# GpSimd's two additions of x's halves in eight pieces, and the last output tile's second product in two pieces of columns

## The chip, the cores and the metric

The kernel runs on one core of a Trainium2 chip. The metric is the device time of one execution in microseconds (us). Engine names are those of the profile: PE is TensorE, PEld its weight loads, DVE is VectorE, ACT is ScalarE, POOL is GpSimd, and SP is the engine that issues most of the DMAs.

## What is computed

An attention layer with a learned position bias (2 batches, 8 heads, 576 positions, head size 64) is followed by a mixture of 4 experts over the 1152 tokens. Cut to what matters:

```python
def _moe_ref(x, domain_probs, w1, w2):      # x: (1152, 512), the attention's output
    p = domain_probs / (domain_probs.sum(-1, keepdims=True) + 1e-09)
    out = np.zeros((N, D), dtype=np.float32)
    for e in range(E):                       # w1[e]: (512, 1024), w2[e]: (1024, 512)
        h = np.maximum(x @ w1[e], 0.0)
        out += p[:, e:e + 1] * (h @ w2[e])
    return out
```

## The kernel before, in words

The program has two parts, each planned by the class `Plan`: a list of operations with engine, cost, due time and dependences, from which a simulated run writes one fixed order per engine. Every engine then works through its own list in that order; it does not skip an instruction that has to wait.

The first part (to about 218 us) is attention. For each of nine tiles of 128 tokens it makes x, and keeps it as two f16 halves, `xx[:, 0]` (the rounded value) and `xx[:, 1]` (what the rounding lost). The part ends with the first product of the first half-expert ("unit" u = 0): `mm1` (L475 to L477) on two groups of 384 tokens, c = 0 and 1, with four blocks of 128 hidden columns ("ft") each. A block of the result goes through one of three rotating buffers `hf`: ScalarE's `ev_a` (L480, L481) writes relu(h) to `hf` and its f16 value to `hh`, and VectorE's `ev_v` (L484) subtracts the two for the low half. A block's `ev_a` thus needs the `ev_v` of the block three before it. On VectorE these eight subtractions stand in one queue with the preparation of the next unit's weights: scales (L268 to L272), gate (L452), `whi` (L459) and two `wlo` (L463).

The second part (`plan_experts`) makes the second product of unit 0 (`mm2`, L497 to L499), the rest of its first product, and units 1 to 7, whose first product is taken in seven block products from sums of x and of w (`prod`, L594). For the sums of x, GpSimd first adds the two halves of x to one f32 array `xf` (in the trace `xsf`): `x_whole` (L547), one instruction for 640 tokens by 4 blocks of 128 features (128x2560 elements) and one for 512 tokens (128x2048). VectorE's `x_sums` (L544) read all of it. Behind `x_whole` GpSimd makes the sums of w for unit 1 (`w_sums`, L574, four instructions of 512 columns).

`mm2(u, tau)` makes one output tile: 4 blocks ft, 3 matmuls each (high by high, high by low, low by high), into one PSUM bank of 512 columns. `sum_up` (L504 for u = 0, else L506) multiplies by the gate and adds on VectorE; after unit 7 `store` (L512) writes the tile's 128 rows of 512 f32 to HBM. The last tile is unit 7, tau = 8.

Of the kernel before, what the change touches and what calls it, by code (L numbers as in the profile page):

```python
# [12 lines left out]
ALU = mybir.AluOpType  # L13
# [3 lines left out]
B, H, S, D = 2, 8, 576, 64  # L17
NF = 32
E, DM, FF = 4, 512, 1024
P = 128  # L20
NTAU = 9
# [4 lines left out]
NU = 8  # L26
# [129 lines left out]
def tile_attention_moe(ctx: ExitStack, tc: tile.TileContext, qd, kd, vd, cst, ltab, dp, mw1, mw2, out):  # L156
    nc = tc.nc
    V, A, G, T, SP = nc.vector, nc.scalar, nc.gpsimd, nc.tensor, nc.sync
# [11 lines left out]
    gate = keep.tile([P, NTAU, E], F32, name="gate")  # L170
    gs = keep.tile([P, NTAU, 1], F32, name="gs")
    gu = keep.tile([P, 2, NTAU], F32, name="gu")
# [8 lines left out]
    xx = keep.tile([P, 2, 4, NT], F16, name="xx")  # L181
# [12 lines left out]
    xf = pa.tile([P, 512], F32, name="xf")  # L194
# [17 lines left out]
    buf = {}  # L212
# [181 lines left out]
    moe = {"raw": [raw[:, 0], raw[:, 1]], "w": [wa]}  # L394
# [70 lines left out]
    def wpart(u, m, l):  # L465
        return moe["w"][u % 2][:, m].rearrange("p (l k f) -> p l k f", l=2, k=4)[:, l]

    def hpart(u, c, l):
        return hh_[:, (3 * u + c) % 2].rearrange("p (l k t) -> p l k t", l=2, k=4)[:, l]
# [13 lines left out]
    def ev_v(u, c, ft, ps, f):  # L483
        V.tensor_tensor(out=hpart(u, c, 1)[:, ft], in0=f, in1=hpart(u, c, 0)[:, ft], op=ALU.subtract)  # L484

    def mm2(u, tau, ps):
        if u:
            i = tau // 5
            hh, hl = hpair(i, 0), hpair(i, 1)
            ts = slice(P * (tau - 5 * i), P * (tau - 5 * i) + P)  # L490
        else:
            c, tt = divmod(tau, 3)
            hh, hl = hpart(u, c, 0), hpart(u, c, 1)
            ts = slice(P * tt, P * tt + P)
        wh, wl = wpart(u, 1, 0), wpart(u, 1, 1)
        for ft in range(4):
            T.matmul(ps, hh[:, ft, ts], wh[:, ft], start=(ft == 0), stop=False)  # L497
            T.matmul(ps, hh[:, ft, ts], wl[:, ft], start=False, stop=False)  # L498
            T.matmul(ps, hl[:, ft, ts], wh[:, ft], start=False, stop=(ft == 3))  # L499

    def sum_up(u, tau, ps):
        g, acc = gu[:, u % 2, tau:tau + 1], moe["acc"][:, tau]
        if u == 0:
            V.tensor_scalar(out=acc, in0=ps, scalar1=g, scalar2=None, op0=ALU.mult)  # L504
        else:
            V.scalar_tensor_tensor(out=acc, in0=ps, scalar=g, in1=acc, op0=ALU.mult, op1=ALU.add)  # L506

    def store(tau):
        acc = moe["acc"][:, tau]
        if tau:  # L510
            r = (tau - 1) % 2 * S + (tau - 1) // 2 * P
            SP.dma_start(out=out[r:r + P], in_=acc)  # L512
        else:
            for b in range(B):
                SP.dma_start(out=out[b * S + 512:b * S + S], in_=acc[64 * b:64 * b + 64])
# [14 lines left out]
    def hpair(i, l):  # L530
        return moe["hp"][i][:, l]

    def tokens(i, t=None):
        o, n = PAIRS[i]
        return slice(o, o + 2 * n) if t is None else slice(o + n * t, o + n * t + n)

    def x_sums(i):

        f = moe["xf"]

        def q(t, a):
            return f[:, 2 * a:2 * a + 2, tokens(i, t)]

        return [lambda x=x: V.tensor_tensor(out=x[0], in0=x[1], in1=x[2], op=x[3]) for x in ((q(1, 1), q(1, 0), q(1, 1), ALU.add), (q(1, 0), q(0, 0), q(1, 0), ALU.subtract), (q(0, 0), q(1, 1), q(0, 0), ALU.subtract), (q(0, 1), q(0, 1), q(0, 0), ALU.subtract))]  # L544

    def x_whole(i):
        G.tensor_tensor(out=moe["xf"][:, :, tokens(i)], in0=xx[:, 0, :, tokens(i)], in1=xx[:, 1, :, tokens(i)], op=ALU.add)  # L547

    def x_halves(i, a, l):
        s = slice(2 * a, 2 * a + 2)  # L550
        f, xs = moe["xf"][:, s, tokens(i)], moe["xs"][:, :, s, tokens(i)]
        if l:
            V.tensor_tensor(out=xs[:, 1], in0=f, in1=xs[:, 0], op=ALU.subtract)
        else:
            A.activation(out=xs[:, 0], in_=f, func=AF.Copy)
# [40 lines left out]
    def plan_experts():  # L596
# [4 lines left out]
        buf = {}  # L601
        EV = -6.0

        def op(name, eng, at, cost, fn, choice=False, **kw):
            plan.add(name, name[0], at, (lambda e: fn(e)) if choice else (lambda e: fn()), cost=cost if choice else {eng: cost}, **kw)
# [33 lines left out]

        def second(u, tau, at):  # L640
            i = tau // 5
            if u:
                deps = [("lo", u, i, k) for k in range(8)] + ([("wlo", u, j) for j in range(2)] if u > 1 else [])
            else:
                deps = [("ev_v", ft) for ft in range(4)] if tau > 5 else []
            op(("mm2", u, tau), "T", at, 2.6, lambda: mm2(u, tau, buf["o", u, tau]), deps=deps, new=[("o", ("o", u, tau))])
            op(("sum", u, tau), "V", at + 2.6 + EV, 0.75, lambda: sum_up(u, tau, buf["o", u, tau]), deps=[("mm2", u, tau)] + ([("gate", u)] if u > 1 else []), use=[("o", u, tau)], after=[("sum", u - 1, tau)] if u else [])
            if u == NU - 1:
                op(("store", tau), "S", at, 1.0, lambda: store(tau), deps=[("sum", u, tau)])
# [47 lines left out]


        for i in range(2):
            op(("xw", i), "G", 6.0 * i, 6.0 - i, lambda i=i: x_whole(i))  # L700
            for k, fn in enumerate(x_sums(i)):
                op(("xs", i, k), "V", 1 + 12.0 * i + k, 0.85, fn, deps=[("xs", i, k - 1)] if k else [("xw", i)])
            for a in range(2):
                op(("xhh", i, a), "A", 4 + 12.0 * i, 1.2, lambda i=i, a=a: x_halves(i, a, 0), deps=[("xs", i, 3)])
                op(("xh", i, a), "V", 5 + 12.0 * i, 1.45, lambda i=i, a=a: x_halves(i, a, 1), deps=[("xhh", i, a)])
        for tau in range(6):
            second(0, tau, 2.6 * tau + (8 if tau > 2 else 0))
        for ft in range(4):
            at = 7.8 + 2 * ft
# [3 lines left out]
        for u in range(1, NU):  # L713
            weights(u)
            a0 = 42.0 * u - 18
            for q in range(2):
                quad(u, 0, q, a0 + 11 * q, 11 / 7.0)
                quad(u, 1, q, a0 + 22 + 10 * q, 10 / 7.0)
            last = range(6, NTAU) if u == 1 else range(5, NTAU)
            for k, tau in enumerate(last):  # L720
                second(u - 1, tau, a0 + 22.0 * (k + 1) / (len(last) + 0.5))
            for k in range(5):
                second(u, k, a0 + 22 + 20.0 * (k + 1) / 5.5 if u < NU - 1 else a0 + 42 + k)
# [44 lines left out]
    for tau in range(NTAU):  # L768
# [4 lines left out]
        for hp in range(HP):  # L773
            p = HP * tau + hp
            op("scores", (p,), 2 * p + PR["scores"], scores, p, deps=[("load_q", tau)] + [("load_k", b, hp) for b in batches], after=chain("scores", p) + [("bias_mm", 8 * block + 3)], new=[("b2", ("s", 2 * p)), ("b2", ("s", 2 * p + 1))], use=[("q", tau)], mode="row2" if tau else "quad")
            for h in range(2):
                u = 2 * p + h
# [4 lines left out]
        for g in range(9):  # L782
            ps = sorted({HP * tau + (4 * g + i) // 9 for i in range(4)})
            at = 2 * ps[-1] + (4 * g + 3) % 9 * 0.1
# [46 lines left out]
    for c in range(2):  # L831
        for ft in range(4):
            for kt in range(4):
                key = ("h", c, ft)
                prev = ("mm1", c, ft, kt - 1) if kt else ("mm1", c, ft - 1, 3) if ft else ("mm1", c - 1, 3, 3) if c else None
                op("mm1", (c, ft, kt), PR["mm1"] + 4 * c + ft, lambda c=c, ft=ft, kt=kt, key=key: mm1(0, c, ft, buf[key][:, 0:384], [kt]),
                   new=[] if kt else [("b1", key)], use=[key] if kt else [], after=[prev] if prev else [],
                   deps=[("xlo", 3 * c + i) for i in range(3)] + [("wlo", 0, j) for j in range(2)])
# [3 lines left out]
    with tc.manual_schedule():  # L842
        load_consts()
        warm()
        prep_consts()
        plan.run()
        plan.emit(buf)
        open_a()
        plan_experts()
# [68 lines left out]
```

## Time and profile before

| | |
|---|---|
| median of three runs (lowest to highest) | 566.19 us (565.79 to 566.46) |
| the profiled execution's own time | 566.17 us |
| its span in the trace | 564.4 us |
| busy share of PE, DVE, ACT, POOL | 96%, 72%, 52%, 26% |
| PE's share of the chain that ended last | 87% |

The span runs from the first to the last instruction of the trace, and 1.77 us of the execution's time lie around it. A row of the timeline gives start, duration, engine, line, operation, and in brackets how long the engine stood idle before it and what ended that. The duration of an instruction runs from its start on the engine to its end, and takes in what it waited for after it started.

### The profile page before, as it was taken

How to read it: one execution, taken by the hardware profiler on the slowest of the kernel's cores; microseconds unless marked ns; L12 is line 12 of the kernel's file. 1: busy time of each engine (PE TensorE's matmuls, PEld its weight loads, DVE VectorE, ACT ScalarE, POOL GpSimd, SP SyncE). 2: the span in 40 equal slices, each digit the busy share in tenths (PEclk: the TensorE clock that was granted, in tenths of full speed). 3: DMA queues.
4: the chain of work that ended last, by engine and by line, in shares of the span. 5: the costliest groups of instructions: out<-in, count | busy, mean ns of one | idle time of the engine just before them, and what ended most of it. 6: DMA issues, size and time to landing. Idle time of an engine off the chain costs nothing.

```text
span 564.4 us, 11030 instructions
## 1 busy us (share of the span) xinstructions
PE 542.4 (96%) x4354; PEld 341.4 (60%) x4354; DVE 408.4 (72%) x829; ACT 293.8 (52%) x611; POOL 146.3 (26%) x156
## 2 busy tenths in 40 slices
PE   8769999999999995999999999999999999999997
PEld 3236667777777852547556565665665665565753
DVE  7658887878889496887795976967958957534532
ACT  5568888787787541625534544544334533423410
POOL 0000000000000082007263471371642624322310
PEclk9799999999999997999999999999999999999999
DMA  6984332132441102021041311410312210000022
GB/s 210 235 279 136 105 122 79 62 104 71 138 148 39 11 1 74 1 75 11 14 136 11 115 35 11 149 11 17 135 10 75 75 11 1 2 1 0 1 76 93
DMA packets 22020, 40.63 MB, mean 72 GB/s; under 512 B 3024, under 2 KB 4048, under 8 KB 21968
## 3 DMA queue, kind: packets, MB, share of 16 engines
q1 hardware_dynamic: 21680, 39.33, 23.9%
q8 instruction: 34, 0.56, 0.4%
q10 hardware_dynamic: 288, 0.59, 0.3%
q14 instruction: 18, 0.15, 0.1%
HBM read 25.75 MB, written 2.37 MB: 50 GB/s over the span
## 4 chain that ended last, share of the span: by engine, by line
PE 87%; DVE 5%; DMA 4%; ACT 2%; issue 1%; SPq 0%; ACTq 0%; DVEq 0%
PE bank L594 24%; PE bank L497 11%; PE bank L499 11%; PE bank L498 11%; PE bank L350 7%; PE bank L318 7%; PE bank L335 7%; PE bank L291 5%; PE bank L361 2%; DMA biasA<-obr 1%; DMA biasB<-obr 1%; DVE hh L484 1%; DMA vv<-vd 1%; DVE wb L463 1%; PE bank L231 1%
## 5 line engine op out<-in xcount | busy, mean ns | idle before, releaser
L677 POOL TENSOR_TENSOR hp<-hf,hp 128x320 f16<-128x320 f32 (+1 forms) x112 | 92.1, 838 | 203.4 <-ACT hf L676 202.4
L594 PEld LDWEIGHTS <-wn 128*128 128x128 f16 x1176 | 115.0, 98 | 40.4 <-issue 1.7
L675 ACT ACTIVATE hp<-xsf 128x320 f16<-128x320 f32 (+1 forms) x112 | 49.0, 437 | 137.9 <-DVE xsf L665 137.4
L665 DVE SCALAR_TENSOR_TENSOR xsf<-bank,xsf 128x320 f32<-128x320 f32 (+1 forms) x196 | 82.4, 451 | 25.6 <-PE bank L594 18.4
L594 PE MATMUL bank<-xs,wn 128*128 128x320 f16 (+1 forms) x672 | 98.2, 286 | 1.0 <-ACT xsf L685 0.6
L506 DVE SCALAR_TENSOR_TENSOR acc<-bank,gu,acc 128x512 f32<-128x512 f32 x63 | 47.1, 747 | 66.9 <-PE bank L499 66.9
L594 PE MATMUL bank<-xx,wn 128*128 128x320 f16 (+1 forms) x504 | 75.5, 286 | 0.0
L330 ACT ACTIVATE er<-er,mr 128x576 f32<-128x576 f32 x72 | 55.2, 769 | 10.6 <-DVE mr L326 10.4
L286 DVE TENSOR_SCALAR fr<-lt,npt 128x576 f32<-128x576 f32 x117 | 52.9, 514 | 5.7 <-PE bank L291 5.4
L497 PE MATMUL bank<-wb,hp 128*128 128x512 f16 x144 | 54.6, 379 | 0.0
L498 PE MATMUL bank<-wb,hp 128*128 128x512 f16 x144 | 54.6, 379 | 0.0
L499 PE MATMUL bank<-wb,hp 128*128 128x512 f16 x144 | 54.6, 379 | 0.0
L318 PE MATMUL bank<-ks,qr 64*128 64x288 f32 (+1 forms) x320 | 47.2, 427 | 5.1 <-ACT obr L294 2.4
L291 PE MATMUL bank<-fr,cs 128*32 128x288 f32 x576 | 44.4, 434 | 3.8 <-ACT obr L294 3.2
L676 ACT ACTIVATE hf<-xsf 128x320 f32<-128x320 f32 (+1 forms) x112 | 47.8, 427 | 0.2 <-POOL hp L677 0.2
L339 ACT ACTIVATE etr<-bank 128x512 f32<-128x512 f32 x69 | 37.5, 596 | 16.6 <-PE bank L335 15.3
L350 PE MATMUL bank<-etr,vv 128*64 128x128 f32 (+1 forms) x800 | 45.5, 265 | 0.0
L350 PEld LDWEIGHTS bank<-etr,vv 128*64 128x64 f32 x800 | 39.6, 137 | 8.6 <-issue 6.8
L499 PEld LDWEIGHTS <-hp 128*128 128x128 f16 x252 | 24.7, 98 | 29.7
L335 PE MATMUL bank<-ident,er 128*128 128x128 f32 x324 | 42.1, 278 | 0.0
L335 PEld LDWEIGHTS bank<-ident,er 128*128 128x128 f32 x324 | 34.8, 141 | 12.0 <-issue 8.4
L497 PE MATMUL bank<-wa,hp 128*128 128x512 f16 x108 | 40.9, 379 | 0.0
(104 smaller groups left out, 763.8 us busy)
## 6 DMA issues: line engine op xcount, KB each, us to landing
raw<-mw SPq DMA_DIRECT2D x32, 512.0 KB
biasB<-obr SPq DMA_DIRECT2D x32, 144.0 KB
biasA<-obr SPq DMA_DIRECT2D x32, 144.0 KB
vv<-vd SPq DMA_DIRECT2D x8, 320.0 KB
ks<-kd SPq DMA_DIRECT2D x8, 288.0 KB
qr<-qd SPq DMA_DIRECT2D x9, 256.0 KB
biasA<-obr SPq DMA_DIRECT2D x8, 288.0 KB
out<-acc SPq DMA_DIRECT2D x8, 256.0 KB
```

Source lines behind the costliest of these rows:

```text
L286: ENG[e].tensor_scalar(out=f, in0=src, scalar1=npt[:, g:g + 1], scalar2=None, op0=ALU.max)
L291: T.matmul(buf["pb", n][32 * t:32 * t + 32, half, 0:288], W2, buf["f", n, t][:, 288 * half:288 * half + 288], start=True, stop=True)
L318: T.matmul(s_out(2 * p + h, c0, c1, half), q[r, c0:c1], ks[r, HP * b + hp, 288 * half:288 * half + 288], start=True, stop=True)
L330: A.activation(out=ehalf(u), in_=ehalf(u), func=AF.Exp, scale=-1.0, bias=buf["m", u // 2][:, u % 2:u % 2 + 1], accum_out=buf["sum", tau][: ...
L335: T.transpose(buf["t", tau, g][:, P * i:P * i + P], buf["e", HP * tau + hp][:, P * j:P * j + P], ident)
L350: T.matmul(x[64 * h:64 * h + 64, P * hp + c0:P * hp + c1], vv[:, HP * b + hp, 5 * h + i], buf["et", tau, g][:, P * j + c0:P * j + c1], sta ...
L497: T.matmul(ps, hh[:, ft, ts], wh[:, ft], start=(ft == 0), stop=False)
L498: T.matmul(ps, hh[:, ft, ts], wl[:, ft], start=False, stop=False)
L499: T.matmul(ps, hl[:, ft, ts], wh[:, ft], start=False, stop=(ft == 3))
L594: T.matmul(ps, w[lw][:, k], x[:, lx, k], start=k == 0 and lw + lx == 0, stop=k == 1 and lw == 1)
L665: V.scalar_tensor_tensor(out=tmp(name), in0=ps(a), scalar=2.0 ** -HS, in1=tmp(other), op0=ALU.mult, op1=ALU.add)
L677: op(("lo", u, i, x), "G", at + pos + EV, 0.2 + 0.6 * r, lambda: G.tensor_tensor(out=lo, in0=buf[f][:, 0:n], in1=hi, op=ALU.subtract), dep ...
```

## The change

`x_whole` takes a block k of 128 features too, and adds 128x640 or 128x512 elements: eight instructions in place of two. The first `x_sums` of a token group depends on all four pieces of it. `mm2`, `sum_up` and `store` take a range of columns; for the last tile alone they are called for columns 0 to 319 and then for columns 320 to 511, each piece with a PSUM bank of its own. A pair of matmul and weight load is there for each piece, so this tile has 24 of them in place of 12.

```diff
-    def mm2(u, tau, ps):
+    def mm2(u, tau, ps, o=slice(0, DM)):
...
-            T.matmul(ps, hh[:, ft, ts], wh[:, ft], start=(ft == 0), stop=False)
-            T.matmul(ps, hh[:, ft, ts], wl[:, ft], start=False, stop=False)
-            T.matmul(ps, hl[:, ft, ts], wh[:, ft], start=False, stop=(ft == 3))
+            T.matmul(ps[:, o], hh[:, ft, ts], wh[:, ft, o], start=(ft == 0), stop=False)
+            T.matmul(ps[:, o], hh[:, ft, ts], wl[:, ft, o], start=False, stop=False)
+            T.matmul(ps[:, o], hl[:, ft, ts], wh[:, ft, o], start=False, stop=(ft == 3))
-    def sum_up(u, tau, ps):
-        g, acc = gu[:, u % 2, tau:tau + 1], moe["acc"][:, tau]
+    def sum_up(u, tau, ps, o=slice(0, DM)):
+        g, acc, ps = gu[:, u % 2, tau:tau + 1], moe["acc"][:, tau, o], ps[:, o]
...
-    def store(tau):
-        acc = moe["acc"][:, tau]
+    def store(tau, o=slice(0, DM)):
+        acc = moe["acc"][:, tau, o]
...
-            SP.dma_start(out=out[r:r + P], in_=acc)
+            SP.dma_start(out=out[r:r + P, o], in_=acc)
...
-    def x_whole(i):
-        G.tensor_tensor(out=moe["xf"][:, :, tokens(i)], in0=xx[:, 0, :, tokens(i)], in1=xx[:, 1, :, tokens(i)], op=ALU.add)
+    def x_whole(i, k):
+
+        G.tensor_tensor(out=moe["xf"][:, k, tokens(i)], in0=xx[:, 0, k, tokens(i)], in1=xx[:, 1, k, tokens(i)], op=ALU.add)
...
+            if (u, tau) == (NU - 1, NTAU - 1):
+
+                for k, o in enumerate((slice(0, 320), slice(320, DM))):
+                    key = (u, tau, k)
+                    op(("mm2",) + key, "T", at, 1.3, lambda o=o, key=key: mm2(u, tau, buf[("o",) + key], o), deps=[("lo", u, i, x) for x in range(8)] + [("wlo", u, j) for j in range(2)] + ([("mm2", u, tau - 1)] if not k else [("mm2", u, tau, 0)]), new=[("o", ("o",) + key)])
+                    op(("sum",) + key, "V", at + 2.6 + EV, 0.45, lambda o=o, key=key: sum_up(u, tau, buf[("o",) + key], o), deps=[("mm2",) + key, ("gate", u)], use=[("o",) + key], after=[("sum", u - 1, tau)])
+                    op(("store",) + key, "S", at, 0.5, lambda o=o: store(tau, o), deps=[("sum",) + key])
+                return
...
-            op(("xw", i), "G", 6.0 * i, 6.0 - i, lambda i=i: x_whole(i))
+            for k in range(4):
+                op(("xw", i, k), "G", 6.0 * i, 1.4 - 0.2 * i, lambda i=i, k=k: x_whole(i, k))
...
-                op(("xs", i, k), "V", 1 + 12.0 * i + k, 0.85, fn, deps=[("xs", i, k - 1)] if k else [("xw", i)])
+                op(("xs", i, k), "V", 1 + 12.0 * i + k, 0.85, fn, deps=[("xs", i, k - 1)] if k else [("xw", i, x) for x in range(4)])
```

GpSimd's list at the turn from the first part to the second (`xx` and `xf` there are attention's, `xsf` is the array of sums, `raw` and `wt` are weights), before:

```order
L380 TENSOR_TENSOR xx<-xf,xx 128x4x128 x2
L547 TENSOR_TENSOR xsf<-xx 128x4x640
L547 TENSOR_TENSOR xsf<-xx 128x4x512
L574 TENSOR_TENSOR wt<-raw 128x512
L574 TENSOR_TENSOR raw<-raw 128x2x256
L574 TENSOR_TENSOR wt<-raw,wt 128x512 x2
```

and with the change, where the lines behind it have moved down by one:

```order
L380 TENSOR_TENSOR xx<-xf,xx 128x4x128 x2
L548 TENSOR_TENSOR xsf<-xx 128x640 x4
L548 TENSOR_TENSOR xsf<-xx 128x512 x4
L575 TENSOR_TENSOR wt<-raw 128x512
L575 TENSOR_TENSOR raw<-raw 128x2x256
L575 TENSOR_TENSOR wt<-raw,wt 128x512 x2
```

The two long rows became four and four; what stands ahead of them and behind them kept its place.

VectorE's list at the end of the program (`bank` is PSUM, `acc` the output tiles), before:

```order
L665 SCALAR_TENSOR_TENSOR xsf<-bank,xsf 128x320
L665 SCALAR_TENSOR_TENSOR xsf<-bank,xsf 128x256 x10
L506 SCALAR_TENSOR_TENSOR acc<-bank,gu,acc 128x512
L665 SCALAR_TENSOR_TENSOR xsf<-bank,xsf 128x256 x4
L506 SCALAR_TENSOR_TENSOR acc<-bank,gu,acc 128x512 x8
```

and with the change:

```order
L674 SCALAR_TENSOR_TENSOR xsf<-bank,xsf 128x256 x10
L506 SCALAR_TENSOR_TENSOR acc<-bank,gu,acc 128x512
L674 SCALAR_TENSOR_TENSOR xsf<-bank,xsf 128x256 x4
L506 SCALAR_TENSOR_TENSOR acc<-bank,gu,acc 128x512 x7
L506 SCALAR_TENSOR_TENSOR acc<-bank,gu,acc 128x320
L506 SCALAR_TENSOR_TENSOR acc<-bank,gu,acc 128x192
```

The last sum became two. PE's last twelve pairs of weight load and 128x512 matmul likewise became twelve with 320 columns and then twelve with 192, and SP's last store two stores. On all other places the lists of all engines are those of before; one ScalarE copy (the second L555) has a further wait, for GpSimd.

## Rows read from the trace of the kernel before

**Rows 1.** The page's fourth part: the chain that ended last, shares by engine.

```profile
PE 87%; DVE 5%; DMA 4%; ACT 2%; issue 1%; SPq 0%; ACTq 0%; DVEq 0%
```

**Rows 2.** PE's timeline: one matmul after the idle time, one ten later.

```profile
218.39 0.59 PE L497 MATMUL bank<-wa,hh 128*128 128x512 f16 x1 [6.67 <-ACT hh L481]
...
222.54 0.38 PE L498 MATMUL bank<-wa,hh 128*128 128x512 f16 x1
```

**Rows 3.** Who waited for whom, PE: total us, times, longest us; after 250 us.

```profile
PE bank L594 <- ACT xsf L685: 0.6, 2, 0.3
```

**Rows 4.** VectorE's timeline from 199 to 219 us; small scale instructions left out.

```profile
199.01 0.56 DVE L484 TENSOR_TENSOR hh<-hf,hh 128x384 f16<-128x384 f32 x1
...
200.96 3.91 DVE L484 TENSOR_TENSOR hh<-hf,hh 128x384 f16<-128x384 f32 x1 [0.24 <-ACT hh L481]
...
205.60 3.22 DVE L452 TENSOR_SCALAR gu<-gate,ws 128x9 f32<-128x9 f32 x1
208.73 0.54 DVE L484 TENSOR_TENSOR hh<-hf,hh 128x384 f16<-128x384 f32 x1
209.20 1.75 DVE L459 TENSOR_SCALAR wb<-raw,ws 128x1024 f16<-128x1024 f32 x1
210.88 2.29 DVE L463 SCALAR_TENSOR_TENSOR wb<-raw,ws,wb 128x1024 f16<-128x1024 f32 x1
...
216.83 2.10 DVE L484 TENSOR_TENSOR hh<-hf,hh 128x384 f16<-128x384 f32 x4
```

**Rows 5.** Line 547: durations in ns (min/median/max), first and last start.

```profile
L547 POOL TENSOR_TENSOR xsf<-xx x2: 4379/4756/5133, 199.3 to 204.4; 128x2560 f32<-128x2560 f16 x1, 128x2048 f32<-128x2048 f16 x1
```

**Rows 6.** GpSimd's timeline behind the two additions.

```profile
208.75 1.65 POOL L574 TENSOR_TENSOR wt<-raw 128x512 f32<-128x512 f32 x1
210.48 1.60 POOL L574 TENSOR_TENSOR raw<-raw 128x512 f32<-128x512 f32 x1
212.04 3.78 POOL L574 TENSOR_TENSOR wt<-raw,wt 128x512 f32<-128x512 f32 x2
```

**Rows 7.** GpSimd's timeline later: instructions of 256, 320 and 512 columns.

```profile
286.49 0.67 POOL L677 TENSOR_TENSOR hp<-hf,hp 128x256 f16<-128x256 f32 x1 [0.95 <-ACT hf L676]
289.39 0.79 POOL L677 TENSOR_TENSOR hp<-hf,hp 128x320 f16<-128x320 f32 x1 [2.23 <-ACT hf L676]
290.14 1.27 POOL L574 TENSOR_TENSOR wt<-raw 128x512 f32<-128x512 f32 x1
```

**Rows 8.** PE's timeline early on: two shorter idle times.

```profile
21.83 6.39 PE L291 MATMUL bank<-fr,cs 128*32 128x288 f32 x48 [2.91 <-ACT obr L294]
...
32.18 1.19 PE L318 MATMUL bank<-ks,qr 64*64 64x288 f32 x12 [1.35 <-ACT obr L294]
```

**Rows 9.** Busy us per stretch (PE, PEld, DVE, ACT, POOL), PEclk, DMA share, GB/s.

```profile
21.00:22.00 1.00, 0.17 (x4) 0.17 (x8) 0.00 (x0) 0.97 (x2) 0.00 (x0) 0.54 0.99 242
...
32.00:33.00 1.00, 0.82 (x12) 0.49 (x12) 0.00 (x0) 1.00 (x4) 0.00 (x0) 1.00 0.51 200
```

**Rows 10.** PE's timeline: the first and last of the last tile's twelve matmuls.

```profile
557.77 0.38 PE L497 MATMUL bank<-wb,hp 128*128 128x512 f16 x1
...
560.14 0.38 PE L499 MATMUL bank<-wb,hp 128*128 128x512 f16 x1
```

**Rows 11.** PE's timeline: two neighbouring groups of six matmuls of 320 columns.

```profile
251.50 0.98 PE L594 MATMUL bank<-xx,wn 128*128 128x320 f16 x6
252.31 0.98 PE L594 MATMUL bank<-xs,wn 128*128 128x320 f16 x6
```

**Rows 12.** Groups of PEld and DVE instructions by form: busy us, mean ns.

```profile
L594 PEld LDWEIGHTS <-wn 128*128 128x128 f16 x1176 | 115.0, 98 | 40.4 <-issue 1.7
...
L665 DVE SCALAR_TENSOR_TENSOR xsf<-bank,xsf 128x256 f32<-128x256 f32 x98 | 37.5, 416 | 8.9 <-PE bank L594 4.8 <-ACT xsf L685 3.6
```

**Rows 13.** VectorE's timeline: the last sum.

```profile
560.56 0.75 DVE L506 SCALAR_TENSOR_TENSOR acc<-bank,gu,acc 128x512 f32<-128x512 f32 x1 [1.84 <-PE bank L499]
```

**Rows 14.** The stretch with the last store's data, columns as in rows 9.

```profile
562.00:563.00 1.00, 0.00 (x0) 0.00 (x0) 0.00 (x0) 0.00 (x0) 0.00 (x0) 1.00 0.70 262
```

## The prediction, on record before the changed kernel was run

> **What bounds the kernel now.** I read the chain that ended last first: PE holds 87% of it [rows 1], so nearly everything else is hidden behind matmuls, and a change pays only where PE stands idle or behind the last matmul. PE's timeline then shows one long idle time after the start of the program: 6.67 us before 218.39 us, which began at 211.72 and was ended by ScalarE's L481 [rows 2]. It costs more than its length: the ten matmuls from 218.39 to 222.54 took 4.15 us, where matmuls of this size stand 0.2155 us apart at the end of the program (557.77 to 560.14 for eleven steps [rows 10]), 2.16 us for ten. TensorE's clock was at its lower level of 1.2 GHz there, and that took another 2.0 us. After 250 us PE's waits are tenths of a microsecond [rows 3], so what PE gains at 218 us should reach the end.
>
> The wait is for ScalarE's last `ev_a` of the first part, which waits for a free `hf` buffer, that is for the fifth `ev_v` on VectorE, the first of the four from 216.83 (0.53 us each, so its end is 217.36) [rows 4]. From there to PE's start are 1.03 us. So I look at VectorE from 199 to 217 us, and what is to be seen is that instructions with two SBUF operands, or with a fast mode, take far longer than their size. The second L484 takes 3.91 us where the first takes 0.56, and the gate (nine elements a partition) 3.22 us [rows 4]. Their ends give the reason. GpSimd's two additions start at 199.3 and 204.4 and last 5.13 and 4.38 us [rows 5], so they end near 204.45 and 208.78. The L484 ends at 204.87, 0.4 us after the first; the gate at 208.82, 0.04 us after the second. The two engines exclude one another: the VectorE instruction waits until the running GpSimd instruction is done. Behind the additions they take turns: L459 ends 0.55 us after GpSimd's first subtraction (210.95 against 210.40), L463 1.09 us after the second (213.17 against 212.08) [rows 4, 6], and the second subtraction ends 1.13 us after L459, 0.14 us less than its undisturbed 1.27 [rows 7].
>
> **The change, part one: eight additions.** The order on VectorE, ScalarE and PE is the same; GpSimd's two instructions become eight. Undisturbed, GpSimd needs 0.67 us for 256 columns and 0.79 for 320 [rows 7], 1.9 ns a column; so 1.39 us for 640 and 1.15 for 512 (the same line gives 4.99 us for the 2560 columns, measured 5.13). Behind a VectorE instruction I take 0.14 less, 1.25 and 1.01. With strict turns, one piece and one VectorE instruction:
>
> - the first L484 ends at 199.57, the first piece at 200.82, the second at 202.21 (the second L484 comes at 200.96, when that piece is running), this L484 at 202.61;
> - third piece 203.86; the gate, ready 0.73 us after that L484 as before, and the third L484 right behind it as before, together 0.5: 204.36;
> - fourth piece 205.61, L459 206.16; fifth 207.17, L463 208.26; sixth 209.27, the fourth L484 209.67; seventh 210.68, L463 211.77; eighth 212.78, the fifth L484 213.18.
>
> Before it was 217.36, so 4.2 us are won. PE starts at 214.2 in place of 218.39, after 2.5 us of idle time. PE's own last matmul of the first part, at 211.72, is the floor.
>
> What is late next: GpSimd's additions end 4 us later, and its four subtractions alternate with the last L484s and end at 212.78 plus four times 1.53, near 218.9. The sums of x on VectorE stand behind the first output tiles (PE's start plus 2.6 us, 216.8 or later) and find the additions done. The first weight part on VectorE may wait up to 1.1 us for the last subtraction; VectorE waits for PE in this stretch anyway. I cost both at nothing; without that cover it would be up to 1.1 us.
>
> **The clock.** The trace has two shorter idle times of PE. In the one of 2.91 us (to 21.83) the clock fell: the mean of that microsecond is 0.54. After the one of 1.35 us it was 1.00 [rows 8, 9]. The new one, 2.5 us, is nearer to the first, though there PE had only scattered small matmuls ahead of it and here 15 us without a gap. I take the fall, at the old price, so no change; the other end is that the 2.0 us go too.
>
> **Part two: the last tile in two pieces.** Twelve matmuls of 320 columns at 0.135 us (0.81 for six [rows 11]) take 1.62 us. For 192 columns the line through 512 and 320 (0.42 ns a column) gives 0.081 us; the upper end is 0.135, that of 320. One weight load takes 98 ns [rows 12], hidden beside the larger matmuls; I take 0.09. The last matmul then starts 1.62 + 11 x 0.09 = 2.61 us after the tile's first, before 2.37: +0.24 (ends +0.14 and +0.73). It is shorter by 0.13 (0.25 for 0.38). The last sum had 0.75 us for 512 columns [rows 13], 256 columns take 0.416 [rows 12]; the line gives 0.33 for 192, so -0.42 (other end -0.33). The sum and the store of the first piece run beside the second piece's matmuls. The last store's data took 0.70 us of DMA time for 256 KB [rows 14]; 96 KB in proportion is 0.26: -0.44, other end 0, since rows of 768 bytes are not in the trace. Together 0.24 - 0.13 - 0.42 - 0.44 = -0.75, ends -0.85 and +0.27.
>
> The Trainium skill's page "TensorE: Matmul & The Clock Gate", section "Back-to-back issue gap", gives for sustained pairs of load and matmul about 131 ns at 512 columns and 81 ns at 128; on a line between them 320 and 192 columns would cost an estimated 106 and 89, so that the divided tile would be 12 x (106 + 89 - 131) = 770 ns longer and the tail would gain nothing. The trace does not agree: 215.5 ns at 512, 135 at 320, and so the rows decide.
>
> **The sum.** The profiled execution took 566.17 us, 0.02 under the median of the runs. 566.17 - 4.2 - 0.75 = 561.2 us.
>
> **The rivals.**
> - *The clock does not fall.* The 2.5 us lie between a case that fell and one that didn't; 15 us of dense work ahead speak for it. 559.2 us.
> - *The gate's turn goes the other way.* The third L484 followed the gate with no piece between, by hundredths of a microsecond (208.73 against GpSimd's 208.75 [rows 4, 6]). If a piece comes between, each later instruction meets the next one, and the fifth L484 waits for a subtraction too: 1.1 us more, 562.3 us.
> - *GpSimd keeps the memory port* (slower). If its next instruction, already queued, is served before a waiting VectorE instruction, the eight pieces and four subtractions run through: 199.57 + 1.25 + 3 x 1.39 + 4 x 1.15 + 4 x 1.27 = 214.7. VectorE then needs 0.4 + 0.73 + 0.5 + 0.55 + 1.09 + 0.4 + 1.09 + 0.4 = 5.2 us to the fifth L484: 219.9, 2.5 later than before, and 567.9 us with the tail. It decides once four or more extra pieces (1.2 us each) pass a waiting instruction. Against it: at 204.45, 210.40 and 212.08 VectorE got in each time.
> - *The pieces do not help*, the long waits having another cause than the additions: only the tail is left, 565.4. Against it stand the matching ends.
>
> **How the numbers follow.** Forecast 0.36; clock stays up 0.30; gate's turn 0.20; no help 0.05; GpSimd keeps the port 0.04; more than summed (PE starts near its floor, clock up) 0.05. The range takes in the first three with the tail's ends: 558.6 to 563.0; the forecast's own is 560.4 to 562.0. About 0.2%, 1.1 us, can be told from no change here. Faster by more: 0.36 + 0.30 + 0.20 + 0.05 = 0.91; the same 0.05; slower 0.04.
>
> **What would show it.** In the new trace the second L484 should end near 202.6 and the gate near 203.9, GpSimd's pieces should last 1.2 to 2.4 us with VectorE instructions between them, PE should start at 214.2, and its matmuls in the 4 us behind should stand 0.43 us apart (clock down) or 0.2155 (up). The tail: 192-column matmuls 0.08 to 0.1 us apart, a last sum of 0.33 us. The forecast is wrong if PE starts after 216 us, if VectorE's order of turns differs, or if new PE waits show between 220 and 260 us.

## The result, and the profile after

| | before | with the change |
|---|---|---|
| median, four executions each | 566.24 us (565.79 to 566.46) | 560.40 us (559.27, 559.61, 561.19, 561.58) |
| ratio, with its 95% interval | | 0.9898 (0.9873 to 0.9924) |
| profiled execution, its span | 566.17, 564.4 us | 559.27, 557.5 us |

The change makes the kernel 5.8 us faster, 1.0%. The forecast was 561.2 us, in a range of 558.6 to 563.0. The four times of the changed kernel lie at two places, two near 559.4 and two near 561.4, and the median between them; the experiments return to that.

VectorE's timeline of the changed kernel, small scale instructions left out (line numbers behind `x_whole` are one higher or more), answers to [rows 4]:

```profile
201.00 1.64 DVE L484 TENSOR_TENSOR hh<-hf,hh 128x384 f16<-128x384 f32 x1 [0.24 <-ACT hh L481]
...
203.37 0.55 DVE L452 TENSOR_SCALAR gu<-gate,ws 128x9 f32<-128x9 f32 x1
203.84 0.54 DVE L484 TENSOR_TENSOR hh<-hf,hh 128x384 f16<-128x384 f32 x1
204.31 1.88 DVE L459 TENSOR_SCALAR wb<-raw,ws 128x1024 f16<-128x1024 f32 x1
206.11 2.17 DVE L463 SCALAR_TENSOR_TENSOR wb<-raw,ws,wb 128x1024 f16<-128x1024 f32 x1
208.21 1.50 DVE L484 TENSOR_TENSOR hh<-hf,hh 128x384 f16<-128x384 f32 x1
209.63 2.17 DVE L463 SCALAR_TENSOR_TENSOR wb<-raw,ws,wb 128x1024 f16<-128x1024 f32 x1
211.73 6.12 DVE L484 TENSOR_TENSOR hh<-hf,hh 128x384 f16<-128x384 f32 x4
```

The second L484 takes 1.64 us in place of 3.91 and the gate 0.55 in place of 3.22, but L459 and the L463s take about what they took: each still waits for one GpSimd instruction, now a piece of an addition and before a subtraction. The last four L484s take 6.12 us in place of 2.10, because the weight subtractions now run beside them. GpSimd's timeline answers to [rows 5, 6]:

```profile
199.36 13.45 POOL L548 TENSOR_TENSOR xsf<-xx 128x640 f32<-128x640 f16 x8 [9.91 <-DVE xx L380]
212.78 1.57 POOL L575 TENSOR_TENSOR wt<-raw 128x512 f32<-128x512 f32 x1
```

The additions take 13.45 us in place of 9.5. By the prediction's prices eight pieces alone would take an estimated 10.2 us (four at 1.39, four at 1.15); the rest is GpSimd waiting for VectorE. PE's waits below show nothing that waits for their end. PE's timeline, to be read beside [rows 2]:

```profile
214.25 0.38 PE L497 MATMUL bank<-wa,hh 128*128 128x512 f16 x1 [2.49 <-ACT hh L481]
...
216.40 0.38 PE L498 MATMUL bank<-wa,hh 128*128 128x512 f16 x1
...
222.01 0.33 PE L475 MATMUL bank<-xx,wa 128*128 128x384 f16 x1
```

and the last of these in the kernel before:

```profile
228.16 0.33 PE L475 MATMUL bank<-xx,wa 128*128 128x384 f16 x1
```

PE starts 4.14 us earlier, after 2.49 us of idle time, and in this execution the next ten matmuls take 2.15 us, not 4.15: the clock stayed at 2.4 GHz. PE's waits after 220 us are two groups as short as before; the first is the one of [rows 3]:

```profile
PE bank L595 <- ACT xsf L694: 0.6, 2, 0.3
PE bank L595 <- DVE xsf L674: 0.4, 2, 0.2
```

The tail, PE's first matmul of each piece and the very last one, and VectorE's two sums, to be read beside [rows 10, 13]:

```profile
551.62 0.30 PE L497 MATMUL bank<-wb,hp 128*128 128x320 f16 x1
...
553.25 0.25 PE L497 MATMUL bank<-wb,hp 128*128 128x192 f16 x1
...
554.16 0.25 PE L499 MATMUL bank<-wb,hp 128*128 128x192 f16 x1
```

```profile
553.46 0.55 DVE L506 SCALAR_TENSOR_TENSOR acc<-bank,gu,acc 128x320 f32<-128x320 f32 x1 [0.88 <-PE bank L499]
554.45 0.42 DVE L506 SCALAR_TENSOR_TENSOR acc<-bank,gu,acc 128x192 f32<-128x192 f32 x1 [0.44 <-PE bank L499]
```

From the tile's first matmul to the span's end it is 5.88 us (551.62 to 557.5); before it was 6.63 (557.77 to 564.4). The span's gain of 6.9 us in these two profiles is thus 4.14 from PE's earlier start, 2.0 of clock and 0.75 of tail. The medians differ by less, 5.8 us: this profile is of an execution at the lower of the two places.

### The profile page after: what moved, and what is told of

Read it like the earlier page. It is cut to its first block, busy times and chain, and to the rows that moved or that the text cites. A ratio compares the mean times of both kernels' runs of the same rounds, so it can differ in the third digit from the quotient of the medians.

```text
span 557.5 us, 11064 instructions
## 1 busy us (share of the span) xinstructions
PE 540.8 (97%) x4366; PEld 342.1 (61%) x4366; DVE 407.9 (73%) x830; ACT 294.2 (53%) x611; POOL 149.6 (27%) x162
## 4 chain that ended last, share of the span: by engine, by line
PE 87%; DMA 5%; DVE 3%; ACT 2%; issue 1%; SPq 1%; ACTq 0%; DVEq 0%
PE bank L595 25%; PE bank L497 11%; PE bank L499 11%; PE bank L498 11%; PE bank L350 7%; PE bank L318 7%; PE bank L335 7%; PE bank L291 5%; PE bank L361 2%; DMA qr<-qd 1%; DMA biasB<-obr 1%; DMA biasA<-obr 1%; DMA vv<-vd 1%; DVE wb L463 1%; DVE hh L484 1%
## 5 line engine op out<-in xcount | busy, mean ns | idle before, releaser
L506 DVE SCALAR_TENSOR_TENSOR acc<-bank,gu,acc 128x512 f32<-128x512 f32 (+1 forms) x64 | 47.3, 740 | 66.4 <-PE bank L499 66.3
L497 PE MATMUL bank<-wb,hp 128*128 128x512 f16 (+2 forms) x148 | 55.2, 373 | 0.0
L498 PE MATMUL bank<-wb,hp 128*128 128x512 f16 (+2 forms) x148 | 55.2, 373 | 0.0
L499 PE MATMUL bank<-wb,hp 128*128 128x512 f16 (+2 forms) x148 | 55.2, 373 | 0.0
L291 PE MATMUL bank<-fr,cs 128*32 128x288 f32 x576 | 45.7, 438 | 4.0 <-ACT obr L294 3.2
L499 PEld LDWEIGHTS <-hp 128*128 128x128 f16 x256 | 25.0, 98 | 29.4
L497 PE MATMUL bank<-wa,hp 128*128 128x512 f16 x108 | 40.9, 379 | 0.0
```

The lines of the kernel that those rows point to most:

```text
L291: T.matmul(buf["pb", n][32 * t:32 * t + 32, half, 0:288], W2, buf["f", n, t][:, 288 * half:288 * half + 288], start=True, stop=True)
L497: T.matmul(ps[:, o], hh[:, ft, ts], wh[:, ft, o], start=(ft == 0), stop=False)
L498: T.matmul(ps[:, o], hh[:, ft, ts], wl[:, ft, o], start=False, stop=False)
L499: T.matmul(ps[:, o], hl[:, ft, ts], wh[:, ft, o], start=False, stop=(ft == 3))
```

## The experiments

Every kernel was timed beside the kernel before on the same chip. There the kernel before had medians of 566.4 to 566.7 us, and its single executions lay between 565.3 and 568.5; so times of one execution are read with care, and the traces carry the weight.

**Each part alone.** The first kernel keeps the eight additions and leaves the last tile whole:

```diff
-            if (u, tau) == (NU - 1, NTAU - 1):
...
-                return
...
```

> Only the eight additions; the last tile whole as before. Theory (the two parts add up): PE starts at 214.2 us as in the changed kernel, and from the last tile's first matmul to the span's end it is 6.6 us as before, 0.75 more than in the changed kernel; 560.1 us with the clock up and 562.1 with it down. Rival (the gain at 214 us is partly due to the tail, or the tail's gain is not its own): a start or a tail off these by over 0.2 us.

560.94 us (560.40 to 562.52), ratio 0.9905 (0.9883 to 0.9927). In its profile PE's idle time is 2.48 us, and this time the clock fell:

```profile
214.03 0.58 PE L497 MATMUL bank<-wa,hh 128*128 128x512 f16 x1 [2.48 <-ACT hh L481]
...
223.32 0.33 PE L475 MATMUL bank<-xx,wa 128*128 128x384 f16 x1
```

The 36 matmuls of L497 to L499 take 9.29 us to the first L475, where the changed kernel takes 7.76 (214.25 to 222.01) and the kernel before took 9.77 (218.39 to 228.16). The stretches of this kernel (PE, PEld, DVE, ACT, POOL, then the granted clock, DMA share, GB/s) show when:

```profile
213.00:214.00 1.00, 0.00 (x0) 0.00 (x0) 1.00 (x2) 0.90 (x3) 1.00 (x1) 0.86 0.77 274
214.00:215.00 1.00, 0.97 (x3) 0.40 (x3) 1.00 (x2) 0.58 (x1) 0.92 (x2) 0.50 0.58 221
...
217.00:218.00 1.00, 1.00 (x6) 0.49 (x5) 0.63 (x1) 0.00 (x0) 0.92 (x2) 0.93 0.00 0
```

The clock fell before 214 us and was back just after 217; the 36 matmuls lost 1.5 us by it. From the last tile's first matmul (552.92) to the span's end it is 6.6 us, as expected, and PE's start agrees too (214.03, with attention 0.2 us earlier than in the changed kernel's profile): the tail's gain belongs to the divided tile.

The second kernel keeps the two long additions and divides the tile:

```diff
-            for k in range(4):
-                op(("xw", i, k), "G", 6.0 * i, 1.4 - 0.2 * i, lambda i=i, k=k: x_whole(i, k))
+            op(("xw", i), "G", 6.0 * i, 6.0 - i, lambda i=i: x_whole(i))
...
```

> Only the divided last tile; GpSimd's two long additions as before. Theory: PE's idle time is 6.7 us and its ten slow matmuls are there; the tail is 5.9 us in place of 6.6; 565.4 to 565.5 us, a ratio of 0.9987. Rival (the tail's gain comes only with the rest): 566.2 us, no difference.

566.01 us against 566.39, ratio 0.9986 (0.9976 to 0.9997): a small gain, and its interval holds the expected 0.9987. PE's idle time is again

```profile
218.78 0.59 PE L497 MATMUL bank<-wa,hh 128*128 128x512 f16 x1 [6.67 <-ACT hh L481]
```

and the tail is 5.8 us (557.78 to 563.6). In the traces the parts add up; the medians leave the tail's part less sharp, since single executions of one kernel differ by more than it.

**The length of a piece.** Four pieces, then sixteen, each with the tail divided:

```diff
-    def x_whole(i, k):
+    def x_whole(i, a):
+        k = slice(2 * a, 2 * a + 2)
...
-            for k in range(4):
-                op(("xw", i, k), "G", 6.0 * i, 1.4 - 0.2 * i, lambda i=i, k=k: x_whole(i, k))
+            for a in range(2):
+                op(("xw", i, a), "G", 6.0 * i, 2.7 - 0.4 * i, lambda i=i, a=a: x_whole(i, a))
...
```

> The additions in four pieces (two blocks of features each, 128x1280 and 128x1024) in place of eight; the tail divided as in the change. Theory (the engines take strict turns, one GpSimd instruction and one VectorE instruction): the second L484 ends at 202.45 us, the gate and the third L484 near 205.4, then the third and fourth piece and three of the weight subtractions each hold up one instruction; the fifth L484 ends near 216.3 and PE starts near 217.3, with the clock down behind 5.6 us of idle time; 564.3 us. Rival (a wait is in proportion to a piece's length, no turns): half way between two and eight pieces, PE at 216.3 or earlier and about 563 us. Rival (other cause than the length): PE at 214.2 as with eight pieces.

564.24 us (563.68 to 567.09), ratio 0.9970 (0.9956 to 0.9984). The profiled execution is the longest of its runs, 2.85 us above the median; its attention part was 2.5 us late (the first L484 starts at 201.49, in the kernel before at 199.01). So I read from that L484's end, 202.05:

```profile
203.44 1.49 DVE L484 TENSOR_TENSOR hh<-hf,hh 128x384 f16<-128x384 f32 x1 [0.24 <-ACT hh L481]
...
207.34 0.55 DVE L484 TENSOR_TENSOR hh<-hf,hh 128x384 f16<-128x384 f32 x1
```

The second L484 ends 2.88 us later (204.93) and the third 5.84 us later (207.89). The expectation had 2.88 and about 5.8, counted from 199.57. PE's row bears it out: idle for 5.57 us against an expected 5.6, and then the lower clock (0.43 us from one matmul's start to the next).

```profile
219.77 0.58 PE L497 MATMUL bank<-wa,hh 128*128 128x512 f16 x1 [5.57 <-ACT hh L481]
```

A wait in proportion to the length would have left 4.6 us or less. Taking turns explains why four pieces win so little: VectorE's first two waits shrink, but of the others, which had each met a subtraction of 1.27 us, two now meet a longer addition and two a subtraction, and the fifth L484, which had met none, meets the third subtraction.

```diff
-    def x_whole(i, k):
+    def x_whole(i, k, t):
...
-            for k in range(4):
-                op(("xw", i, k), "G", 6.0 * i, 1.4 - 0.2 * i, lambda i=i, k=k: x_whole(i, k))
+            for k in range(4):
+                for t in range(2):
+                    op(("xw", i, k, t), "G", 6.0 * i, 0.7 - 0.1 * i, lambda i=i, k=k, t=t: x_whole(i, k, t))
...
```

> The changed kernel with the additions in sixteen pieces (128x320 and 128x256). Theory (turns, a wait of at most 0.65 us each): the fifth L484 ends near 210.1 us, before PE's last block is done (211.75), so PE's own product is the floor: PE starts near 212.8 us after 1.05 us of idle time, and the clock stays up in every run; 557.8 us, all runs within 0.5 us. Rival (the fixed cost of GpSimd's instructions eats it, 0.19 us each): PE not before 214 us, and 559 us or more. Rival (later stall: the weight sums end near 220 us and hold up the first products): PE starts at 212.8 but new PE waits show before 255 us and the time is 559 us.

558.05 us (557.37 to 558.87), ratio 0.9845 (0.9827 to 0.9864), the best version with the last one below. PE's idle time is down to

```profile
213.01 0.38 PE L497 MATMUL bank<-wa,hh 128*128 128x512 f16 x1 [0.96 <-ACT hh L481]
```

against 1.05 expected, and in this profile the clock stays up. The five times spread over 1.5 us, where 0.5 was expected. The sum of the turns was 0.5 us off here: the fifth L484 ends at 210.90, by the expectation near 210.4 (its 210.1, with attention 0.34 us later in this profile). The second L484 started just behind the third piece and waited for the whole of it. Worked out as in the prediction, with pieces of an estimated 0.65 and 0.53 us behind a VectorE instruction, the turns give 210.0 for the fifth L484 if the second comes behind the second piece, and 210.7 if it comes behind the third; 210.56 was measured, without the 0.34:

```profile
201.27 0.78 POOL L547 TENSOR_TENSOR xsf<-xx 128x320 f32<-128x320 f16 x1
```

```profile
201.30 1.17 DVE L484 TENSOR_TENSOR hh<-hf,hh 128x384 f16<-128x384 f32 x1 [0.24 <-ACT hh L481]
```

PE's start doesn't show it, since ScalarE's last copies now wait for PE's own last product and not for a buffer. GpSimd ends its additions and subtractions later still, and PE's waits after 220 us are 0.6 and 0.4 us, as in the kernel before:

```profile
199.66 15.85 POOL L547 TENSOR_TENSOR xsf<-xx 128x320 f32<-128x320 f16 x16 [9.91 <-DVE xx L380]
...
218.37 3.07 POOL L574 TENSOR_TENSOR wt<-raw,wt 128x512 f32<-128x512 f32 x2
```

Here PE's own last block and ScalarE's copies of it are the bound, so at this place finer pieces have nothing left to give.

**The clock.** Was the spread of the changed kernel's times the clock? First it ran again as it is.

> The changed kernel, nothing edited. Theory (PE starts at 214.25 us in every execution, and the clock falls behind its 2.5 us of idle time in some executions and not in others): two clusters of times, near 559.4 and 561.4 us, 2.0 us apart, the upper one with the lower mean granted clock (0.988 against 0.991), and nothing between them. Rival (the spread of the four runs has another cause): times spread evenly, or the clock does not go with the time.

559.40, 559.38, 561.24, 561.16 and 560.69 us: again two places, and one time between where none was expected. The mean clock of the two near 561.2 was 0.991, as of the two near 559.4; only the fifth had 0.987. So the mean clock of a whole execution does not tell the cases apart, and both parts of the expectation fell. Then the idle time was filled, first in the changed kernel with ten matmuls, then in the kernel before with 28:

```diff
         plan.emit(buf)
+        for i in range(10):
+            T.matmul(bank[:, i % 2, :], wa[:, 0, 0:128], wa[:, 0, 0:512], start=True, stop=True)
         open_a()
```

> The changed kernel with ten more matmuls of 512 columns on PE in the idle time (results unused, 2.2 us at full rate). Theory (the spread of the changed kernel is the clock's fall behind the idle time): PE's first L497 stays at 214.2 to 214.3 us, no matmul behind it is slow, and all runs are at the lower cluster, 559.3 to 559.7 us. Rival (the spread comes from elsewhere): two clusters remain.

559.51, 559.54, 559.76 and 559.56 us: in these four executions the upper place is gone. PE's first L497 waits 0.32 us and runs at the full rate, as all behind it:

```profile
211.85 2.32 PE L859 MATMUL bank<-wa 128*128 128x512 f16 x10
214.49 0.38 PE L497 MATMUL bank<-wa,hh 128*128 128x512 f16 x1 [0.32 <-ACT hh L481]
```

> The kernel before with 28 more matmuls of 512 columns in its 6.67 us of idle time (results unused, 6.0 us at full rate). Theory (the clock's fall costs 2.0 us there, apart from the wait): PE's first L497 stays near 218.4 us, the matmuls behind it stand 0.2155 us apart, 564.2 us. Rival (the slow matmuls are not due to the idle time): 566.2 us.

564.21 us, ratio 0.9956 (0.9944 to 0.9968), 1.8 to 3.2 us; the expected 2.0 lies within. Ten matmuls take 2.16 us:

```profile
217.58 0.38 PE L497 MATMUL bank<-wa,hh 128*128 128x512 f16 x1 [0.65 <-ACT hh L481]
...
219.74 0.38 PE L498 MATMUL bank<-wa,hh 128*128 128x512 f16 x1
```

Attention was 0.82 us earlier in this profile (its last L367, VectorE's first step for the last tile of x, starts at 196.31 us, in the kernel before at 197.13). With that the wait ends when it ended (217.58 and 218.39), and only the clock is different: from L367's start to the span's end it is 365.3 us in place of 367.3. So the fall was worth 2 us here, apart from the wait.

Last, three more profiles of the changed kernel, a, b and c, to split its spread.

> The changed kernel, nothing edited, one more profile. Theory: its times differ by two things. The start of the program, measured by the start of the last attention tile's L367 on VectorE, shifts from execution to execution (196.3 to 199.6 us in the profiles so far); and the clock falls or stays up behind the 2.5 us of idle time. From L367's start to the span's end it should then be 360.3 us with the clock up, and 361.8 to 362.3 where it fell. Rival (something else varies too): other values than these.

> As the look before: from L367's start to the span's end 360.3 us with the clock up behind the idle time, 361.8 to 362.3 where it fell; the rest of the time's spread is the start of L367. Rival: other values.

> As the two looks before: 360.3 us from L367's start to the span's end with the clock up, 361.8 to 362.3 where it fell. Rival: other values.

| changed kernel, profile | time us | L367 starts | from there to the span's end | 36 matmuls L497 to L499 |
|---|---|---|---|---|
| first | 559.27 | 197.17 | 360.3 | 7.76 |
| run again | 559.40 | 197.31 | 360.3 | 7.77 |
| a | 561.02 | 197.46 | 361.8 | 9.24 |
| b | 559.00 | 196.92 | 360.3 | 7.77 |
| c | 560.70 | 196.93 | 362.0 | 9.45 |

Two of these five executions lost 1.5 and 1.7 us to the clock, and the rest of their spread is the start of L367, that is attention. The values are the expected ones. For the longer executions without a profile (560.69 to 561.58 us) it is not shown how much of their length is clock and how much attention. The idle time of PE is 2.48 or 2.49 us in all five. In a the clock fell in the idle time, in c only when PE had been running again for half a microsecond; c's stretches, beside those of b, where the clock stayed up:

```profile
213.00:214.00 1.00, 0.00 (x1) 0.00 (x1) 1.00 (x1) 0.93 (x3) 1.00 (x1) 1.00 0.81 299
214.00:215.00 1.00, 1.00 (x4) 0.43 (x4) 1.00 (x2) 0.55 (x1) 0.92 (x2) 0.74 0.39 148
215.00:216.00 1.00, 1.00 (x4) 0.29 (x2) 1.00 (x2) 0.00 (x0) 1.00 (x2) 0.50 0.00 0
```

```profile
214.00:215.00 1.00, 1.00 (x5) 0.48 (x5) 1.00 (x2) 0.55 (x1) 0.92 (x2) 1.00 0.44 168
215.00:216.00 1.00, 1.00 (x7) 0.46 (x5) 1.00 (x2) 0.00 (x0) 1.00 (x2) 1.00 0.00 0
```

The traces also show what sets the price of a fall. At 1.2 GHz the matmuls stand 0.43 us apart and at 2.4 GHz 0.2155, twice as close, so the loss should be half of the time for which PE runs at the lower level. When the clock was back is worked out from the mean of the microsecond in which it rose (0.76 from 222 us means 0.48 us at half speed, so 222.5):

```profile
222.00:223.00 1.00, 1.00 (x5) 0.37 (x4) 0.00 (x0) 0.00 (x0) 0.00 (x0) 0.76 0.00 0
```

| profile | PE runs at 1.2 GHz, us | half of it | lost by the 36 matmuls (over 7.77) |
|---|---|---|---|
| kernel before | 218.39 to 222.5 | 2.0 | 2.0 |
| tail only | 218.78 to 222.1 | 1.7 | 1.6 |
| four pieces | 219.77 to 224.5 | 2.4 | 2.3 |
| eight pieces, whole tile | 214.03 to 217.1 | 1.6 | 1.5 |
| changed kernel, a | 214.53 to 217.5 | 1.5 | 1.5 |
| changed kernel, c | 214.5 to 217.9 | 1.7 | 1.7 |

So a fall has no fixed price; with the long wait as it was it cost 2.0 us in one profile and 1.6 in another.

**Shorter matmuls.** The last question is the price of a matmul narrower than any in the kernel before. To the sixteen pieces a third piece of the last tile was added:

```diff
-                for k, o in enumerate((slice(0, 320), slice(320, DM))):
+                for k, o in enumerate((slice(0, 256), slice(256, 416), slice(416, DM))):
...
```

> Sixteen additions, and the last tile in three pieces of 256, 160 and 96 columns in place of 320 and 192. Question: does the weight load of 98 ns set the pace of short matmuls? Theory (it is hidden, columns decide): 96-column matmuls stand about 0.043 us apart, 160-column ones 0.069; the three pieces take 12 x (0.109 + 0.069 + 0.043) = 2.65 us, the last sum is 0.1 us shorter than with 192 columns (0.32), and from the tile's first matmul to the span's end it is 5.7 us in place of 5.9; about 557.9 us. Rival (the load sets the pace): 96-column matmuls 0.098 us apart, the tail 0.6 us longer than by the theory, 6.3 us, and 558.5 us.

557.96 us (557.62 to 558.19), ratio 0.9851 (0.9835 to 0.9868); against two tail pieces the difference is too small for the times to show. The trace shows it: the last twelve matmuls, of 96 columns, from the first to the last in eleven steps,

```profile
552.91 0.21 PE L497 MATMUL bank<-wb,hp 128*128 128x96 f16 x1
...
553.38 0.21 PE L499 MATMUL bank<-wb,hp 128*128 128x96 f16 x1
```

stand 0.043 us apart, while their weight loads are recorded with 98 ns each. The load does not set the pace. The tail is 5.6 us (550.77 to 556.4), 5.7 expected.

## Why the prediction was right, point by point

- *Turns of VectorE and GpSimd, 4.2 us.* Shown. The measured ends are 202.64, 204.38, 206.19, 208.28, 209.71 and 211.80 us for the second and third L484, L459, L463, the fourth L484 and L463; the working had 202.61, 204.36, 206.16, 208.26, 209.67 and 211.77, counted from a first L484 that ended 0.04 us earlier than the measured one. PE starts at 214.25 (214.2). The same rule, worked out beforehand for four pieces, gave an idle time of 5.6 us, and 5.57 was measured. For sixteen pieces the idle time (1.05 expected, 0.96 measured) tests PE's own bound, not the turns.
- *The gate's turn.* The third L484 again followed the gate with no piece between, in all kernels tried. The rival with 562.3 us did not come.
- *GpSimd keeps the port; the pieces don't help.* Neither came: of the GpSimd instructions queued, only the one that was running held up a waiting VectorE instruction.
- *The clock.* This is the weak part of the forecast. It took the fall, by the nearer of two rows, as a little likelier than none (0.36 against 0.30), and at the old price of 2.0 us. The fall came in two of five profiles, so forecast and rival are cases of the same kernel, and that the median, 560.40 us, lies between them is luck: two of the four executions were at each place. Where the clock fell in the changed kernel it cost 1.5 to 1.7 us. The forecast's case came out as 560.7 to 561.0 us in the two profiles that show it, the rival's (559.2) as 559.0 to 559.4 in three. The two rows could not decide it, and they were not read in full. There was a third shorter idle time, of 1.89 us, and the clock stayed up behind it:

```profile
42.04 1.87 PE L318 MATMUL bank<-ks,qr 64*64 64x288 f32 x16 [1.89 <-DVE mr L326]
```

```profile
42.00:43.00 1.00, 0.96 (x8) 0.40 (x12) 1.00 (x3) 0.98 (x3) 0.00 (x0) 1.00 0.78 217
```

PE's work ahead of the 2.91 us was not scattered: it was busy for 0.70 to 1.00 of each microsecond from 12 to 19 us. And the row of 1.35 us, behind which the clock stayed up, is no rule either: in the first profile of the changed kernel that place has an idle time of 1.49 us, and the clock fell.

```profile
32.09 2.18 PE L318 MATMUL bank<-ks,qr 64*64 64x288 f32 x12 [1.49 <-ACT obr L294]
```

```profile
32.00:33.00 1.00, 0.91 (x8) 0.54 (x10) 0.00 (x0) 1.00 (x4) 0.00 (x0) 0.50 0.52 202
```

- *The later cover.* Right in its outcome: GpSimd's subtractions end near 219 us as worked out, and PE has no new wait behind 220 us. The cover was thinner than the reason given for it (VectorE waits for PE there anyway): VectorE's L484s run to 217.85, so its first sum starts only behind them, at 217.77 (an instruction starts up to 0.1 us before the recorded end of the one ahead). That is some 0.7 us after PE's first tile is done, and VectorE is idle again only before 222.21.
- *The tail, -0.75.* Measured -0.75, which is partly luck, since terms were off and offset each other. The last sum starts 2.83 us after the tile's first matmul, 0.04 later than before (0.11 expected), because 192-column matmuls stand 0.083 us apart and not 0.09. The sum takes 0.42 us, not 0.33: the price at 256 columns came from L665's 0.416 us, while L506 itself takes 0.48 us there (the experiment with three pieces), so the wrong row was taken. From the sum's end to the span's end it is 2.6 us in place of 3.1, -0.46 (-0.44 expected for the store's data); with the 48 KB of the third piece it is 2.5. By the sustained spacing that the Trainium skill states (page "TensorE: Matmul & The Clock Gate", section "Back-to-back issue gap"), the last sum would have started an estimated 0.7 us later than before, and by the prediction's other terms the tail would have gained some 0.2 us, not nothing as the prediction has it. The rows at 192, 160 and 96 columns (0.083, 0.069, 0.043 us) follow the columns, and the measurement decides.
- *The range.* Its ends do not follow from the tail's ends exactly (559.2 with -0.85 gives 559.1, 562.3 with +0.27 gives 563.3, where 558.6 and 563.0 stand). Nothing hangs on it here.

## What to carry to other kernels

When two engines exclude one another for whole instructions, the length of the longest instruction on the idle-looking engine is a wait on the busy one: write down both lists in order, let them take turns, and add up. That sum was right to 0.1 us for four and eight pieces. For sixteen it was 0.5 us off, because one instruction just missed its turn, which did not matter there. The sum also says when cutting finer stops paying, here when PE's own work became the bound. Look for such a wait where an engine's instruction takes several times its usual duration and ends just behind another engine's.

## What was not expected

An idle time of PE of one and the same length, 2.49 us, ends with the clock at 1.2 GHz in some executions and at 2.4 in others, and in one of them the fall came when PE was already running again (0.74 in the microsecond from 214 us). An idle time of this length thus has two prices, and one profile shows only one of them. Filling it with matmuls whose results nobody uses bought 559.5 to 559.8 us in four executions of the changed kernel, and some 2 us in the kernel before. What decides between fall and no fall was not found. Also, attention's end shifts between 196.3 and 199.6 us from execution to execution of kernels that do the same until then; why was not tried. The Trainium skill's page "SBUF — State Buffer", section "SBUF: two separate sides", calls the port that VectorE and GpSimd share an exclusive lock for a whole instruction. The traces agree: before, the second L484 started at 200.96 us and ended at 204.87, 0.4 us after the first addition. In these traces the two then take turns while both have such instructions waiting, with one exception that came in every kernel: the nine-element gate and the L484 behind it go in one turn.
